# Moving three groups of loads from one issuing engine's program to another's, ahead of a cast, in a fused attention and gated-MLP kernel

## Chip, core and metric

The kernel runs on one core of a Trainium2 chip. The core has a matrix engine (TensorE, PE in the profile), a vector engine (VectorE, DVE), a scalar engine (ScalarE, ACT), a general engine (GpSimd, POOL) and SyncE (SP), which here only issues transfers. Each engine runs its own instructions in order. Transfers are carried by 16 DMA engines that all the issuing engines share; the profile calls the queue that POOL fills q0 and the one that SP fills q1. The metric is the device time in microseconds (us) of one execution. Before the change it was 238.27 us, the median of three runs (238.08 to 239.02).

## What is computed

Eight batches of grouped attention (16 query heads on 4 key/value heads, 384 positions, width 64), followed by a gated layer with a mixing step over positions:

```python
scores = scale * np.matmul(q, k.transpose(0, 1, 3, 2))
attn = softmax(scores)                       # over the keys
x = np.matmul(attn, v)                       # heads side by side: 8 x 384 x 1024
h = np.maximum(x @ w_in, 0.0)                # 1024 -> 1024
u, v = h[..., :512], h[..., 512:]
v_n = (v - mean(v)) / np.sqrt(var(v) + 1e-06)
v_s = np.einsum('ts,bsd->btd', w_spatial, v_n) + b_spatial[None, :, None]
out = (u * v_s) @ w_out                      # 512 -> 1024
```

All inputs and the output are float32; the kernel computes its matrix products in 16-bit floats.

## The kernel before

Each batch is cut into six sets (three blocks of 128 query positions by two halves of the heads), and each set into three units, one for each block of 128 keys: 18 units a batch, 144 in all. A unit is a pair of score products (tile sc, line 281), whose exponentials ACT takes (aT, line 293). After three units the values are weighted (av, line 301), and DVE divides by the row sums (lines 315 and 317) into x16.

A written plan decides the order of all instructions. The loop over units emits scores and weights; `at(n, f, ...)` books an action for unit n; `pour` fills PE's time between the scores with the matrix products of the gated layer, which the generator `gated` yields one by one. From unit 21 on the loop takes three units at a time (21, 24, 27, ...), so an action booked for 29 is emitted in the block that begins at 27, and one booked for 30, 31 or 32 in the block that begins at 30. Within one block the order of the bookings holds. Each engine then runs what was emitted for it in that order, and waits where its data isn't there.

The gated layer of one batch has these products: pv (line 357, the half that is normalised), pu (438, the half that gates), psp (457, the mixing over positions, which reads the turned spatial weights wsT16), and po (496, the output, which reads w_out16 and the gated tile gT). Between them POOL normalises (vn, line 401) and multiplies u by the mixed v (gT, line 474).

Inputs come as follows:

- `load_k`, `load_v`, `load_q` (lines 116 to 134) bring a batch's keys, values and queries in float32. A batch's queries are two tiles (j = 0, 1) of three blocks of positions each; `ts` says which blocks a load takes, so that the first block, ts = (0,), can come ahead of the "late" ones, (1, 2). The last argument is the engine that issues the transfer, SP if none is given.
- `cast_k`, `cast_v`, `cast_q` (lines 182 to 208) make 16-bit copies, mostly on POOL.
- `k_send`, `q_send` (lines 248 to 262) turn these copies by transposing transfers that SP issues; `x_send` (line 338) does the same with a batch's x16 and `send_spatial` (line 585) with the spatial weights. For the first two batches PE turns k and q itself.
- `load_w_in` and `load_w_out` (lines 161 to 171) are issued by POOL and change the type on the way, so 1 MB of w_out16 is written in two halves of 512 KB.
- `load_spatial` (line 566) brings the bias and the spatial weights on SP's queue; `cast_spatial` (line 573) makes POOL lay out the bias (line 575) and cast the weights in three steps (line 580).

`behind_rest` (line 630, booked for unit 3) is a run of POOL work for the batches ahead, with `cast_spatial` and `send_spatial` at its end. The third batch (b = 2 in the code) is the first whose keys and queries are turned by transfers. Its first score unit is unit 36, and it needs the late query blocks from unit 42 on. Before the change, w_out is loaded by POOL in the block of unit 24, the values and the late queries of the third batch by SP in the blocks of 27 and 30, and their casts stand in the blocks of 33 and 36.

Of the kernel before, what the change touches and what calls it, by code (L numbers as in the profile page):

```python
# [18 lines left out]
def kernel(  # L19
# [18 lines left out]
    DM = moe_w_in.shape[0]  # L38
    DFF = moe_w_in.shape[1]
    DH = DFF // 2  # L40
# [31 lines left out]
    pool, dve, act, sp = nc.gpsimd, nc.vector, nc.scalar, nc.sync  # L72
# [32 lines left out]
    def stage_tile(n, b, j=None):  # L105
        shape = [P, 2, NT, G * D] if n == "q" else [P, HKV, NT * D]
        t = ld.tile(
            shape, FP32, name=f"{n}32_{b}_{j}", tag=f"{n}32", bufs=5 if n == "q" else 2
        )
        stage[n, b, j] = t  # L110
        return t

    def part(src, t, lo, hi, eng):
        eng.dma_start(t[:, lo:hi, :], src[lo:hi].rearrange("h (p t) d -> p h (t d)", t=NT))
# [4 lines left out]
    def load_v(b, eng=sp):  # L119
        part(v[b], stage_tile("v", b), 0, HKV, eng)  # L120

    def part_q(b, j, hs, ts, eng):
        h0, h1, t0, t1 = hs[0], hs[-1] + 1, ts[0], ts[-1] + 1
        eng.dma_start(  # L124
            stage["q", b, j][:, h0:h1, t0:t1],
            q[b, 8 * j + 4 * h0 : 8 * j + 4 * h1].rearrange(
                "(h i) (c t r) d -> (i c) h t (r d)", i=G, t=NT, r=G
            )[:, :, t0:t1],
        )

    def load_q(b, j, eng=sp, ts=(0, 1, 2)):
        if ts[0] == 0:
            stage_tile("q", b, j)
        part_q(b, j, (0, 1), ts, eng)
# [33 lines left out]
    def load_w_out(lo, hi):  # L168
        pool.dma_start(
            w_out16[:, :, lo:hi], moe_w_out[:, lo:hi].rearrange("(m p) f -> p m f", p=P)  # L170
        )
# [401 lines left out]
    def cast_spatial():  # L573
        b32, ws32 = spatial32["b"], spatial32["w"]
        pool.tensor_copy(
            bias_bc.rearrange("a (t r c) -> a t r c", t=NT, r=G),
            b32.rearrange("a (c t r) -> a t r c", t=NT, r=G),
        )
        for tt in range(NT):
            pool.tensor_copy(  # L580
                ws16[:, :, tt].rearrange("p s (r c) -> p s r c", r=G),
                ws32[:, tt].rearrange("p (c s r) -> p s r c", s=NT, r=G),
            )
# [10 lines left out]
    def at(n, f, *args):  # L594
        todo.setdefault(n, []).append((f, args))
# [34 lines left out]
    def behind_rest():  # L630
        load_q(1, 1, pool)
        load_v(1, pool)
        cast_q(0, 1, pool, (2,))
        load_w_in(0, 0, 4)
        load_w_in(0, 4, 8)
        new_spatial()
        pool.memset(spatial32["b"][:, 0:1], 0.0)
        pool.memset(spatial32["w"][:, 0, 0:1], 0.0)
        load_spatial(sp)
        cast_k(1, pool)  # L640
        load_k(2, pool)
        cast_q(1, 0, pool)
        load_q(2, 0, pool, (0,))
        cast_q(1, 1, pool, (0,))
        cast_q(1, 1, pool, (1, 2))
        load_q(2, 1, pool, (0,))
        cast_v(1, pool)
        cast_spatial()
        send_spatial()
# [32 lines left out]
    at(24, q_send, 2, 0, 0, 1)  # L682
    at(26, cast_q, 2, 1, pool, (0,))
    at(26, q_send, 2, 1, 0, 1)
    at(26, load_w_out, 0, DH)
    at(26, load_w_out, DH, DM)
    at(29, load_q, 2, 0, sp, (1, 2))
    at(29, load_v, 2)
    at(31, load_q, 2, 1, sp, (1, 2))
    at(36, cast_v, 2, pool)  # L690
    for j, n in ((0, 34), (1, 36)):
        at(n, cast_q, 2, j, pool, (1, 2))
        at(n + 1, q_send, 2, j, 1, NT)
    at(36, load_k, 3)
# [345 lines left out]
```

## Time and profile before

| | |
|---|---|
| median of three runs | 238.27 us (238.08 to 239.02) |
| the profiled execution | 238.65 us |
| its span, first to last instruction | 237.1 us |
| granted clock of PE | 1.00 |
| PE busy | 230.4 us (97% of the span) |
| ACT busy | 170.0 us (72%) |
| DVE busy | 143.8 us (61%) |
| POOL busy | 102.2 us (43%) |
| DMA | 47.48 MB, mean 200 GB/s |

Busy time is the time in which an engine has an instruction at work; issuing transfers and waiting are not counted. A line of the timeline has the start, the duration, the engine, the line of code, the operation and what it writes from what it reads; in brackets stands how long the engine sat idle before it, and what ended that. The chain of waits is followed back from the last instruction, and lists what released each step. The DMA view of a stretch lists, for each queue, the packets that started in it, their megabytes, and the time that they took as a share of 16 engines; its last lines list the issues of that stretch with the time from issue to landing.

Around the change, POOL lays out the bias at 25.08 us, casts the spatial weights from 29.44 us and issues w_out at 34.14 us. SP issues the turn of the spatial weights at 31.94 us, the first x turn at 33.99, the third batch's k at 35.33, its first query blocks at 37.00 and 40.80, its late queries and values at 42.44, 43.09 and 47.04, and the turns of the late queries at 50.10 and 53.61.

### The profile page before, as it was taken

To read this page: it belongs to the slowest core of one execution; us is meant where nothing else is said; L and a number is where in the kernel's file an instruction comes from. 1 tells how busy PE (TensorE), PEld (TensorE's weight loads), DVE (VectorE), ACT (ScalarE), POOL (GpSimd) and SP (SyncE) were. 2 spreads that over 40 slices of the span, in tenths; PEclk is the share of its full clock that TensorE was granted. 3 is DMA by queue.
4 is the path that set the end of the run, shared out by engine and by line. 5 is a ranking of instruction groups with operands and counts; after the bars stand their busy time and mean duration, and the time that the engine had idled before them with its cause. 6 is when DMAs were issued, how large, how long until landed. Compare 5 with 4: busy or idle time off the path is not lost.

```text
span 237.1 us, 5954 instructions
## 1 busy us (share of the span) xinstructions
PE 230.4 (97%) x2317; PEld 124.3 (52%) x2317; DVE 143.8 (61%) x382; ACT 170.0 (72%) x350; POOL 102.2 (43%) x149
## 2 busy tenths in 40 slices
PE   7899999999999999999999999999999999999993
PEld 6555655545554545555464555554465455545542
DVE  2668774676447674566646576376744667367561
ACT  2899989959897869977797776986697776401212
POOL 3489493642556442275045800575032500460740
PEclk9999999999999999999999999999999999999999
DMA  6999959999999999699988899479912543240266
GB/s 186 289 300 308 275 152 160 169 317 260 296 211 237 258 351 171 214 199 309 188 257 214 241 214 294 68 271 158 255 27 44 114 164 79 48 177 0 86 229 222
DMA packets 67757, 47.48 MB, mean 200 GB/s; under 512 B 48368, under 2 KB 60576, under 8 KB 67728
## 3 DMA queue, kind: packets, MB, share of 16 engines
q1 hardware_dynamic: 62800, 39.86, 68.9%
q0 software_dynamic: 3952, 6.42, 12.3%
q10 hardware_dynamic: 976, 0.82, 1.1%
q8 instruction: 18, 0.29, 0.5%
q14 instruction: 11, 0.09, 0.1%
HBM read 25.95 MB, written 12.58 MB: 163 GB/s over the span
## 4 chain that ended last, share of the span: by engine, by line
PE 91%; DMA 4%; DVE 2%; issue 0%; ACTq 0%; ACT 0%
PE pu L438 18%; PE pv L357 17%; PE po L496 17%; PE sc L281 15%; PE av L301 14%; PE psp L457 7%; DMA q<-in_q_dram 2%; DMA qT<-q 2%; PE qps L240 1%; PE xps L334 1%; DVE x L317 1%; DVE qT L218 0%; DVE osb L218 0%; DVE q L208 0%; ACTq L124 0%
## 5 line engine op out<-in xcount | busy, mean ns | idle before, releaser
L293 ACT ACTIVATE aT<-sc 128x512 f16<-128x512 f32 x288 | 147.5, 617 | 31.4 <-PE sc L281 30.8
L301 PEld LDWEIGHTS <-aT 128*128 128x128 f16 x1152 | 47.0, 97 | 17.3 <-issue 2.3
L357 PE MATMUL pv<-w_in,xt 128*128 128x512 f16 x192 | 51.0, 380 | 0.1
L301 PE MATMUL av<-v,aT 128*128 128x65 f16 x1152 | 50.5, 193 | 0.1
L496 PE MATMUL po<-w_out,gT 128*128 128x512 f16 (+2 forms) x200 | 50.5, 371 | 0.0
L438 PE MATMUL pu<-xt,w_in 128*128 128x384 f16 x256 | 49.9, 327 | 0.0
L401 POOL TENSOR_SCALAR vn<-vr,rstd,nmr 128x512 f16<-128x512 f32 x23 | 17.6, 779 | 67.0 <-DVE nmr L396 45.6
L474 POOL TENSOR_TENSOR gT<-vs,uT 128x384 f16<-128x384 f32 x31 | 32.4, 1058 | 31.8 <-DVE r_all L315 16.9
L317 DVE TENSOR_TENSOR x<-av,r_all 128x256 f16<-128x256 f32 x96 | 40.7, 424 | 3.3
L281 PE MATMUL sc<-qT,kT 64*128 64x512 f16 x288 | 41.5, 380 | 0.3
L315 DVE RECIPROCAL r_all<-av 128x4 f32<-128x4 f32 x96 | 17.1, 178 | 40.6 <-PE av L301 40.3
L218 DVE COPY osb<-po 128x512 f32<-128x512 f32 (+2 forms) x39 | 26.1, 669 | 16.3 <-PE po L496 16.3
L438 PEld LDWEIGHTS <-w_in 128*128 128x128 f16 x256 | 22.1, 98 | 17.1 <-issue 5.5
L449 ACT ACTIVATE uT<-pu 128x384 f16<-128x384 f32 x32 | 15.8, 495 | 16.0 <-PE pu L438 15.8
L496 PEld LDWEIGHTS <-gT 128*128 128x128 f16 x200 | 17.6, 98 | 17.1 <-issue 3.3
L357 PEld LDWEIGHTS <-xt 128*128 128x128 f16 x192 | 15.8, 97 | 17.8 <-issue 5.5
L281 PEld LDWEIGHTS <-kT 64*128 64x128 f16 x288 | 10.9, 94 | 23.5 <-issue 11.9
L457 PE MATMUL psp<-wsT,vn 128*128 128x384 f16 x96 | 22.2, 327 | 0.0
L469 DVE TENSOR_TENSOR vs<-psp,bias_bc 128x384 f32<-128x384 f32 x32 | 17.6, 552 | 7.1 <-PE psp L457 6.9
L371 DVE TENSOR_SCALAR vr<-pv 128x512 f32<-128x512 f32 x24 | 16.4, 682 | 8.4 <-PE pv L357 8.3
L203 POOL CAST q<-q 128x768 f16<-128x768 f32 x22 | 17.6, 830 | 7.9 <-issue 4.3
L383 DVE BATCH_NORM_STATS2 stats<-vr 128x6 f32<-128x512 f32 x24 | 16.4, 685 | 0.1
(55 smaller groups left out, 103.2 us busy)
## 6 DMA issues: line engine op xcount, KB each, us to landing
out_dram<-osb SPq DMA_DIRECT2D x20, 512.0 KB, 3.9
q<-in_q_dram SPq DMA_DIRECT2D x10, 768.0 KB, 5.7
v_None<-in_v_dram SPq DMA_DIRECT2D x6, 384.0 KB, 7.0
w_in<-in_moe_w_in_dram POOLq DMA_DIRECT2D x4, 512.0 KB, 9.8
k_None<-in_k_dram SPq DMA_DIRECT2D x5, 384.0 KB, 3.8
out_dram<-osb SPq DMA_DIRECT2D x7, 256.0 KB, 2.5
q<-in_q_dram POOLq DMA_DIRECT2D x2, 768.0 KB, 7.6
w_out<-in_moe_w_out_dram POOLq DMA_DIRECT2D x2, 512.0 KB, 9.5
```

The lines of the kernel that those rows point to most:

```text
L203: eng.tensor_copy(t16[:, :, :, hh, :], src[:, hh])
L218: (act.copy if eng is act else dve.tensor_copy)(o, i)
L281: nc.tensor.matmul(sc, kTs[b][rows, j, kt * P : (kt + 1) * P], qTs[b, j][rows, qt].rearrange("p (r i c) -> p i r c", r=G, i=G), start=True ...
L293: act.activation(a, sc, AF.Exp, scale=scale)
L301: nc.tensor.matmul(av[:, i * (D + 1) : (i + 1) * (D + 1)], aT[:, kt, hh, i * P : (i + 1) * P], v1[b % 2][:, 2 * j + hh, kt, 0 : D + 1], st ...
L317: dve.tensor_tensor(x16s[b][:, qt, c : c + 256].rearrange("p (i d) -> p i d", i=G), o[:, :, 0:D], r.to_broadcast([P, G, D]), ALU.mult,)
L357: nc.tensor.matmul(pv, xts[b][:, kt, st * P : (st + 1) * P], w_in16[:, kt, DH:DFF], start=(kt == 0), stop=(kt == NK - 1),)
L401: (dve if b == 0 and st == 1 else pool).tensor_scalar(vn, v_r.pop((b, st)), rstd[:, st : st + 1], nmr[:, st : st + 1], op0=ALU.mult, op1=A ...
L438: nc.tensor.matmul(pu[:, 0:S], w_in16[:, kt, m * P : (m + 1) * P], xts[b][:, kt, :], start=(kt == 0), stop=(kt == NK - 1),)
L457: nc.tensor.matmul(psp[:, 0:S], v_n[b, st][:, m * P : (m + 1) * P], wsT16[:, st, :], start=(st == 0), stop=(st == NT - 1),)
L474: pool.tensor_tensor(gT, vs, uT, ALU.mult)
L496: nc.tensor.matmul(po[:, 0:width], gTs[b][:, m, tt * P : (tt + 1) * P], w_out16[:, m, c0 : c0 + width], start=(m == 0), stop=(m == NM - 1),)
```

## The change

```diff
@@ cast_spatial
             bias_bc.rearrange("a (t r c) -> a t r c", t=NT, r=G),
             b32.rearrange("a (c t r) -> a t r c", t=NT, r=G),
         )
+        load_w_out(0, DH)
+        load_w_out(DH, DM)
+        load_v(2, pool)
+        load_q(2, 0, pool, (1, 2))
         for tt in range(NT):
             pool.tensor_copy(
                 ws16[:, :, tt].rearrange("p s (r c) -> p s r c", r=G),
@@ the bookings of the third batch
     at(24, q_send, 2, 0, 0, 1)
     at(26, cast_q, 2, 1, pool, (0,))
     at(26, q_send, 2, 1, 0, 1)
-    at(26, load_w_out, 0, DH)
-    at(26, load_w_out, DH, DM)
-    at(29, load_q, 2, 0, sp, (1, 2))
-    at(29, load_v, 2)
-    at(31, load_q, 2, 1, sp, (1, 2))
-    at(36, cast_v, 2, pool)
-    for j, n in ((0, 34), (1, 36)):
+    at(26, load_q, 2, 1, pool, (1, 2))
+    at(30, cast_v, 2, pool)
+    for j, n in ((0, 31), (1, 36)):
         at(n, cast_q, 2, j, pool, (1, 2))
         at(n + 1, q_send, 2, j, 1, NT)
     at(36, load_k, 3)
```

Four transfers are now issued by POOL between the layout of the bias and the casts of the spatial weights: both halves of w_out (POOL issued them before, too, in the block of 24), the third batch's values, and the late blocks of its first query tile. The late blocks of the second query tile are issued by POOL where w_out stood. SP loses its three loads. The cast of the values goes from the block of 36 to that of 30, the cast of the first query tile's late blocks and their turn from 33 to 30. The second query tile's late cast and turn stay where they were, in the block of 36. No instruction of PE, ACT or DVE is added, removed or moved.

## The prediction

> **What bounds the kernel now.** I read the page's busy line first, then busy time by stretches, then the chain of waits. TensorE (PE) is busy for 230.4 of 237.1 us. In stretches of 2 us it is full from 32 us on, with three exceptions (columns: PE, PEld, DVE, ACT, POOL busy, clock, DMA share, GB/s):
>
> ```profile
> PE 230.4 (97%) x2317; PEld 124.3 (52%) x2317; DVE 143.8 (61%) x382; ACT 170.0 (72%) x350; POOL 102.2 (43%) x149
> ```
> ```profile
> 50.00:52.00 2.00, 1.89 (x21) 0.95 (x18) 1.93 (x6) 1.63 (x4) 0.90 (x2) 1.00 1.13 357
> ...
> 54.00:56.00 2.00, 1.88 (x29) 1.02 (x24) 1.62 (x5) 2.00 (x6) 0.00 (x0) 1.00 0.76 204
> 56.00:58.00 2.00, 1.95 (x20) 1.07 (x20) 1.40 (x5) 2.00 (x6) 0.78 (x2) 1.00 1.17 328
> ```
>
> These three hold 0.28 us of idle. Starts tell more than modelled ends: the last output matmul at 50.53 is followed at 51.02 by the third batch's first av (0.49 us, where its neighbours stand 0.22 apart), which waits for POOL's cast of v; the scores at 55.08 start 0.31 us after the last av, about 0.19 over the usual; four smaller gaps between 54.5 and 56.3 hold some 0.3. Together **0.75 us**, all that faster third-batch data can give. The granted clock is 1.00 there. The chain of waits agrees on the place but overstates the size, because during those 4.94 us PE did other work:
>
> ```profile
> 42.33 0.49 PE psp L457 x3
> ...
> 45.87 1.08 PE pv L357 x5
> ...
> 50.10 4.94 DMA qT<-q
> 55.08 1.13 PE sc L281 x6
> ```
>
> So there is little to win and much to lose: whatever PE needs later than today is added in full. The due times in the PE timeline are 42.16 for the turned spatial weights (wsT, first psp), 45.70 for the turned x, 48.10 for the third batch's kT and qT.
>
> **The change, part by part.** POOL's timeline (start, us, what, idle before):
>
> ```profile
> 25.08 0.87 POOL L575 COPY bias_bc<-spatial 128x384 f32<-128x384 f32 x1
> 29.44 2.47 POOL L580 CAST ws<-spatial 128x384 f16<-128x384 f32 x3 [3.49 <-DMA spatial<-in_moe_w_spatial_dram]
> ...
> 34.14 1.50 POOL L169 DMA_DIRECT2D w_out<-in_moe_w_out_dram  x2
> ```
>
> *Issuing on POOL.* Four issues now stand between the bias copy and the weight casts: two of w_out (1.50 us), one of v (0.78 us at 13.97), one of q (0.71 us at 21.10), sum 2.99. POOL sits idle there for 3.49 us, waiting for the spatial weights, so the issues end near 28.95, before the weights land, and cost 0. If the weights landed at once they would cost 2.99 on wsT. At 34.14 the two w_out issues become one of q: 0.75 us less on POOL. SP loses three issues (0.58, 0.48, 0.58 = 1.64 us at 42.44, 43.09, 47.04); its transposes of x and q stand closer together. PE is not waiting for those issues: 0.
>
> *The casts moved.* Cast of v (0.83 us) moves from 50.14 and the first late q cast (1.17) from 48.91 to just behind the normalisation, which ends at 40.89. This adds a wait: with data late, the gating multiplies (gT, from 43.57) queue behind it on POOL, and the first output matmul at 47.96 behind them. 2.00 us of casts fit in the 2.68 us of idle there, if data is in by about 41.5; if data comes at 45, gT slips by 3.4, of which its lead over PE (the last of four ends at 47.45, PE reads it near 49.3) covers 1.8. The price is 0 to 1.6; I take 0, because the next point delays psp, and so gT, more. The turn of q, sent at 50.10 today and landing at 55.04, can go about 5 us sooner; the stalls at 51.0 and 55.1 go: -0.75, range 0 to -0.75, as nothing else idles there. The second late q part comes from POOL at about 33.4 instead of SP at 47.04; its cast keeps its place (52.41, 1.44 us of wait gone) and PE needs its turn only at 59.61: 0. Nothing is late next, since PE is full behind these stalls.
>
> *The bytes.* This is what I think decides. The w_out transfers move from 34.14 to about 26, with v and both late q parts right behind them on POOL's DMA queue (q0): 1.0 MB written plus 1.31 MB (0.39 + 2 x 0.52). They wait in that queue behind loads that drain near 31. So they run from 31 on, beside the turn of wsT (on SP's queue, q1), issued at 31.94. Today w_out starts after that turn. What the turn does alone, in 33 to 35 us (packets, MB, share; then issues with us to landing):
>
> ```profile
> q1 hardware_dynamic: 1184, 0.30, 77.6%
> ...
> wsT<-ws SPq DMA_TRANSPOSE x1, 4.2
> xt<-x SPq DMA_TRANSPOSE x1, 6.5
> ```
>
> and beside w_out, in 37 to 40 us, then in 40.25 to 44.25 us:
>
> ```profile
> q0 software_dynamic: 450, 0.45, 112.2%
> q1 hardware_dynamic: 39, 0.00, 1.7%
> ```
> ```profile
> q0 software_dynamic: 533, 0.53, 90.8%
> q1 hardware_dynamic: 541, 0.14, 37.6%
> ```
>
> Alone, a turn moves 592 packets of 256 bytes a us; beside w_out 135, one for each packet of w_out (133 a us). (A turn's packets are its bytes by 256: 1152 for wsT, 1024 for x, 768 for kT.) The kT turn, issued at 35.33, thus landed 11.2 us after its issue, where wsT took 4.2.
>
> The estimate for wsT: w_out has 1024 packets (1 MB at 1 KB); from 31.0 to 33.1, when the turn's data starts, it moves 2.1 x 150 = 315 (150 from the 450 in 3 us). The other 709 take 709/133 = 5.3 us, to 38.4, in which wsT moves about as many and has some 440 left. Then 1.31 MB of v and q: q loads alone move 1.36 MB in 16.5 to 20 us, 389 GB/s, so 3.4 us; at some 4 KB a packet they are 320 packets, so 320 of wsT's go between (320/592 = 0.5 us), to 42.3; the last 120 take 0.2: data done at 42.5. From last data to landing is about 1.35 us for wsT today, and 3.3 for the x turn beside w_out (data gone by 37.25, landed 40.5). Near the first, since q0 is empty by then: **44.4**. PE's psp, due at 42.16, stalls **2.2 us**. Bounds: wsT landing as today (36.15, stall 0) and 46.5 as kT did behind all of w_out (4.3). Behind it, x needs 1024/592 = 1.7 us more and lands near 46.5 to 47 (due 45.70 + 2.2 = 47.9), kT and qT follow by 49 (due 50.3): no second stall.
>
> The Trainium skill, "DMA: Bandwidth & Descriptors", section "Queues, rings and completion order", says that an engine takes turns between queues by whole packets, typically 9 to 17 descriptors, before it switches. If a turn of wsT were 13 of its 256-byte pieces, 1152 would need 89 turns, the landing would be near 37, and the time that of the first rival below. The 533 against 541 of today speak for one record against one.
>
> The same section says that a completion's increment lands only after every earlier write of that engine, across its queues. The 3.3 us of the x turn agree with it; by it alone wsT would land not before the writes of v and q, and the sum would be that of the second rival.
>
> **Sum.** 2.2 - 0.75 = +1.45 us. The profiled execution took 238.65 us (span 237.1, 1.55 around it), 0.38 above the median of the runs, so 240.1 on its terms and 238.27 + 1.45 = **239.7** on the median's.
>
> **Rivals.**
> - *The turn is in time.* Point: wsT lands before 42.16. For it: today's slack is 6 us, and an engine may give the turn several packets for one of q0's where q0 holds q and v. Against: the 135 packets a us. Then only the saving is left: 238.27 - 0.75 = 237.5; not slower. Chance 0.25.
> - *The turn lands behind everything.* A landing of 45.8 to 46.5, with x then near 48: stall 3.6 to 4.3, less 0.75: 241.1 to 241.8. For it: the 3.3 us tail and kT's 11.2 us. Against: q0 should be empty by 43. Chance 0.15.
> - *The change does not do what it says.* The third batch's data comes sooner, but its turns still queue behind the earlier ones on SP, so the stalls at 51 and 55 stay; wsT in time: 238.3. Chance 0.06.
> - *POOL's new wait.* wsT in time, v or q late, gT held up to 1.6: 238.3 to 239.1. Chance 0.04.
>
> **Chances and range.** The forecast has 0.50, alone 238.6 to 241.0 (landing 43.3 to 45.7). A difference of 0.5% (1.19 us, beyond 237.08 or 239.46) is about what a measurement of this kernel tells from no change. Slower: 0.37 of the forecast's 0.50 and the second rival's 0.15: 0.52. Faster needs more than the 0.75 us that the gaps hold: 0.05, out of the first rival. Same: the rest, 0.43. The range takes in the first rival below and most of the second above: 237.3 to 242.0.
>
> **What would show it.** Right: wsT's turn landing some 12 us after its issue instead of 4.2; an idle PE ahead of the first psp, near 42 to 44; q1 with about 135 packets a us in 33 to 38; no gaps near 51 and 55 (moved by the stall). POOL's casts of the spatial weights should still start near 29.4. Wrong: wsT landed by 42, PE full through 40 to 58, or casts of the weights that start late because the issues take longer than 0.75 us each.

## The result, and the profile after

The changed kernel takes 242.70 us (median of six executions, 240.69 to 247.56) where the kernel before took 238.42 us in its own six. The ratio is 1.0142, with a 95% interval of 1.011 to 1.0175: 1.4% slower, 241.7 us on the forecast's median. The ratio leaves out two disturbed executions, so it is below the quotient of the medians. The profiled execution took 242.29 us against 238.65, its span is 240.7 us against 237.1.

Busy time is unchanged (PE 230.5 us); the time went into waiting. PE, DVE and the other engines in the stretches around the change (columns as before):

```profile
42.00:44.00 2.00, 0.64 (x8) 0.18 (x4) 0.61 (x2) 1.69 (x4) 1.48 (x3) 1.00 1.38 110
44.00:46.00 2.00, 0.14 (x1) 0.13 (x2) 0.00 (x0) 0.63 (x2) 0.15 (x1) 1.00 1.40 158
...
50.00:52.00 2.00, 2.00 (x21) 0.97 (x21) 1.25 (x4) 1.25 (x3) 2.00 (x4) 1.00 0.97 185
...
58.00:60.00 2.00, 1.89 (x18) 0.72 (x15) 1.97 (x5) 2.00 (x6) 0.00 (x0) 1.00 1.07 230
```

PE, full before in 42 to 46, worked for 0.78 of these 4 us. The chain of waits names what it waited for:

```profile
32.58 13.14 DMA wsT<-ws
45.72 0.14 issue
45.85 0.65 PE psp L457 x3
```

The turn of the spatial weights landed 13.1 us after its issue, where it took 4.2. Laid beside each other instruction by instruction, the two traces of PE stand 0.33 us apart from 16.5 us on (a wait for w_in in this execution, in which the change has no part), 3.69 from the first psp, 3.42 from the third batch's first av, and 3.4 to the end: **+3.36** at the first psp, **-0.27** at the av. In POOL's timeline the new issues cost nothing:

```profile
26.36 1.51 POOL L169 DMA_DIRECT2D w_out<-in_moe_w_out_dram  x2
27.84 0.78 POOL L114 DMA_DIRECT2D v_None<-in_v_dram  x1
28.61 0.72 POOL L124 DMA_DIRECT2D q<-in_q_dram  x1
30.10 2.45 POOL L584 CAST ws<-spatial 128x384 f16<-128x384 f32 x3 [0.77 <-DMA spatial<-in_moe_w_spatial_dram]
```

They end at 29.33, and POOL still waits 0.77 us for the weights. What the DMA queues moved in 33 to 36 us (nothing on q1), in 36.5 to 38.5 us, then in 42.5 to 45 us:

```profile
q0 software_dynamic: 603, 0.60, 121.5%
```
```profile
q0 software_dynamic: 223, 0.53, 96.2%
q1 hardware_dynamic: 193, 0.05, 18.1%
```
```profile
q1 hardware_dynamic: 444, 0.11, 140.8%
q0 software_dynamic: 24, 0.08, 8.3%
```

In the first stretch the turn, though issued at 32.58, moves nothing beside w_out. In the second it again gets about one packet for each of q0's. In the third q0 is all but empty, and still SP's queue moves 178 packets a us instead of 592. Not all of these can be wsT's: q1 had started 936 packets by 42.5 us, wsT's turn has 1152, and the x turn is next in that queue.

### The profile page after: what moved, and what is told of

Its sections match the earlier page's. It is cut to its first block, busy times and chain, and to the rows that moved or that the text cites. A ratio compares the mean times of both kernels' runs of the same rounds, so it can differ in the third digit from the quotient of the medians.

```text
span 240.7 us, 5955 instructions
## 1 busy us (share of the span) xinstructions
PE 230.5 (96%) x2317; PEld 124.2 (52%) x2317; DVE 143.1 (59%) x382; ACT 170.1 (71%) x350; POOL 104.4 (43%) x152
## 4 chain that ended last, share of the span: by engine, by line
PE 85%; DMA 11%; DVE 1%; SPq 1%; issue 0%; POOL 0%
PE po L496 17%; PE pv L357 17%; PE pu L438 16%; PE sc L281 14%; PE av L301 13%; PE psp L457 7%; DMA wsT<-ws 5%; DMA w_in<-in_moe_w_in_dram 4%; DMA v_None<-in_v_dram 2%; PE xps L334 0%; PE qps L240 0%; DVE x L317 0%; SPq L114 0%; DVE osb L218 0%; DVE vr L371 0%
## 5 line engine op out<-in xcount | busy, mean ns | idle before, releaser
L293 ACT ACTIVATE aT<-sc 128x512 f16<-128x512 f32 x288 | 147.6, 618 | 34.3 <-PE sc L281 33.5
L301 PE MATMUL av<-v,aT 128*128 128x65 f16 x1152 | 50.5, 193 | 0.0
L496 PE MATMUL po<-w_out,gT 128*128 128x512 f16 (+2 forms) x200 | 50.5, 371 | 0.0
L438 PEld LDWEIGHTS <-w_in 128*128 128x128 f16 x256 | 22.1, 98 | 17.1 <-issue 5.5
L496 PEld LDWEIGHTS <-gT 128*128 128x128 f16 x200 | 17.6, 98 | 17.1 <-issue 2.8
```

The lines of the kernel that those rows point to most:

```text
L293: act.activation(a, sc, AF.Exp, scale=scale)
L301: nc.tensor.matmul(av[:, i * (D + 1) : (i + 1) * (D + 1)], aT[:, kt, hh, i * P : (i + 1) * P], v1[b % 2][:, 2 * j + hh, kt, 0 : D + 1], st ...
L438: nc.tensor.matmul(pu[:, 0:S], w_in16[:, kt, m * P : (m + 1) * P], xts[b][:, kt, :], start=(kt == 0), stop=(kt == NK - 1),)
L496: nc.tensor.matmul(po[:, 0:width], gTs[b][:, m, tt * P : (tt + 1) * P], w_out16[:, m, c0 : c0 + width], start=(m == 0), stop=(m == NM - 1),)
```

## The experiments

**Theory.** A DMA engine takes a packet from each queue in turn, and turns follow one another on SP's queue; so a turn is late by the packets that POOL's queue holds ahead of it and beside it. **Rivals:** POOL's own time ahead of the casts (place); w_out alone, because it converts its type (kind); the volume alone, whatever its packets and order; and, for the spread of the times, PE's clock. The table has each kernel's median and its ratio to the kernel before on the same chip; "turn" is the time of wsT's turn from issue to landing, "PE waits" the long waits of PE between 40 and 60 us in the profiled execution (e10's was 5.4 us slower than its median).

| kernel | turn, us | PE waits, us | median, us | ratio, 95% interval |
|---|---|---|---|---|
| before | 4.2 | none | 238.42 | |
| changed | 13.1 | psp 3.2 | 242.70 | 1.0142, 1.011 to 1.0175 |
| e1, w_out back | 6.4 | none | 238.86 | 1.0030, 1.0003 to 1.0057 |
| e2, w_out alone ahead | 6.9 | none | 238.33 | 0.9995, 0.9974 to 1.0016 |
| e3, all behind the casts | 11.7 | psp 1.4, pv 0.7 | 239.97 | 1.0061, 1.0025 to 1.0098 |
| e4, changed, idle filled | 14.9 | filled, psp 1.3 left | 243.25 | 1.0200, 1.0158 to 1.0243 |
| e5, e3 in 2 KB packets | 17.1 | psp 5.4 | 245.29 | 1.0262, 1.0213 to 1.0311 |
| e6, e3 in 512 B packets | 7.0 | pv 2.8 | 243.52 | 1.0206, 1.0150 to 1.0262 |
| e7, w_out ahead, rest at 34 | 12.2 | psp 1.0, pv 8.8 | 250.50 | 1.0416, 1.0356 to 1.0476 |
| e8, changed, small ones first | 14.7 | psp 3.9 | 244.42 | 1.0198, 1.0137 to 1.0259 |
| e9, e7 with ACT issuing | 14.1 | psp 3.3 | 243.86 | 1.0200, 1.0138 to 1.0262 |
| e10, psp doesn't need the turn | 16.0 | pv 3.9 | 240.51 | 1.0084, 1.0050 to 1.0119 |
| e11, e5, idle filled | 15.2 | filled | 244.46 | 1.0236, 1.0171 to 1.0301 |
| e12, casts sooner alone | 3.7 | po 4.4 | 245.06 | 1.0281, 1.0232 to 1.0329 |

**e1: w_out back where it was.**

```diff
-        load_w_out(0, DH)
-        load_w_out(DH, DM)
...
     at(26, load_q, 2, 1, pool, (1, 2))
+    at(26, load_w_out, 0, DH)
+    at(26, load_w_out, DH, DM)
```

> Theory (bytes): what delays the turn of the spatial weights is the volume that stands ahead of it on POOL's DMA queue, most of it w_out. With w_out back behind that turn, only 0.91 MB of v and q stay ahead, which the queue moves by about 34; the turn, issued near 32.5, lands by 39, before PE needs it at 42.4. No stall there, the gap before the third batch's first av (0.27 us) stays gone: 237.7 to 238.4, within 0.5% of before. Rival (place): any transfer that POOL issues ahead of its casts of the spatial weights delays them or the turn by the same 3 us: 240.5 or more, and PE idle ahead of the first psp.

The turn landed at 37.1, PE was full through 42 to 54, and the gap before the av was gone. POOL's place ahead of the casts is not what costs: two issues stand there still. The gain of 0.27 us is in the profile, but not in the time, which is 0.3% above before and above what was expected. That is less than the 0.5% that a measurement of this kernel tells from no change.

**e2: w_out alone ahead** (the first hunk's two `load_w_out` lines in the kernel before, and its two bookings at 26 gone).

> Only the two w_out transfers go in front of the casts of the spatial weights; v, late q, their casts and turns are as before. Theory (bytes): w_out alone drains by 38 to 40 (its second half landed at 40.3 in the changed kernel), and the turn of the spatial weights, with 1152 packets, lands at 40 to 42, just before PE needs it: stall 0 to 0.5, the old gaps at 51 and 55 stay, 238.3 to 239.2. Rival (kind of transfer): w_out, which converts its type, is the whole cause, and v and q add nothing: wsT lands near 45, stall 2.5 to 3.4, 241 to 242.5.

The turn landed at 39.8, a little sooner than expected, and PE had no wait at its use, near 43.1 in that execution. w_out alone is harmless, as v and q alone are in e1: it takes both, 1.9 MB ahead of the turn and 0.5 MB beside it. The kind alone is not the cause.

**e3: all four issues right behind the casts of the spatial weights.**

```diff
-        load_w_out(0, DH)
-        load_w_out(DH, DM)
-        load_v(2, pool)
-        load_q(2, 0, pool, (1, 2))
         for tt in range(NT):
...
+        load_w_out(0, DH)
+        load_w_out(DH, DM)
+        load_v(2, pool)
+        load_q(2, 0, pool, (1, 2))
```

> All of the change, but the four transfers are issued right behind the casts of the spatial weights instead of in front of them. Theory (bytes ahead of the turn): the turn of the spatial weights then starts before w_out does and lands by 38; no stall at the first psp. The x turn that follows takes the delay (landing 44 to 47, due 45.9): stall 0 to 1. 237.8 to 239.3. Rival (order does not matter, the same 2.3 MB compete with the same turns): 241 or more.

Half missed: w_out (issued at 31.44) and the turn (31.51) now start together, so the turn has no lead, and lands at 43.2 instead of by 38; the time is 0.7 us above the expected range. The x turn took the delay that was expected (a wait of 0.7). The six us in which both run, 34 to 40, give the cleanest sight of the alternation (packets, MB, share):

```profile
q0 software_dynamic: 926, 0.93, 91.4%
q1 hardware_dynamic: 914, 0.23, 29.6%
```

**e5 and e6: the same place, other packets.** w_out by rows (512 packets of 2 KB), then in four quarters by columns (2048 of 512 bytes):

```diff
 # e5
+        m0, m1 = lo * NM // DM, hi * NM // DM
-            w_out16[:, :, lo:hi], moe_w_out[:, lo:hi].rearrange("(m p) f -> p m f", p=P)
+            w_out16[:, m0:m1], moe_w_out[m0 * P : m1 * P].rearrange("(m p) f -> p m f", p=P)
 # e6
-        load_w_out(0, DH)
-        load_w_out(DH, DM)
+        for c in range(0, DM, 256):
+            load_w_out(c, c + 256)
```

> As the kernel with the four transfers behind the casts (239.97 us, wsT's turn from 31.5 to 43.2), but w_out comes in two halves by rows instead of by columns, so the same 1 MB is 512 packets of 2 KB instead of 1024 of 1 KB. Theory (an engine takes one packet from each queue in turn): the turn of 1152 packets has moved only some 512 when w_out is through, near 41, and needs v's and q's packets and more for the rest: wsT lands at 44.5 to 46, the first psp stalls 2 to 3.5, 241 to 242.5. Rival (the queues share by time or bytes): wsT lands near 43.2 as before, 240.0.

> The same placement, but w_out in four quarters by columns: 2048 packets of 512 bytes, four issues (POOL spends 1.5 us more there). Theory (one packet from each queue in turn): the turn moves its 1152 packets beside as many of w_out's and is done before w_out is: wsT lands at 40.5 to 42.3, no stall or under 0.4 at the first psp; the x turn behind it may still be late by up to 1.5: 238.3 to 240. Rival (share by time or bytes): wsT lands near 43.2 or later, the stall of 1.2 stays.

The landing follows the packets: 47.4 with 2 KB, 43.2 with 1 KB, 38.1 with 512 bytes, for the same megabyte; both changes go the expected way, further than expected. The counts in 38 to 40 us of e5 and in 33 to 35 us of e6 show why: one for one at either size.

```profile
q0 software_dynamic: 174, 0.36, 94.0%
q1 hardware_dynamic: 176, 0.05, 19.1%
```
```profile
q0 software_dynamic: 451, 0.23, 84.8%
q1 hardware_dynamic: 417, 0.11, 40.0%
```

The rival (shares by time or bytes) falls. Both times missed their ranges, e5's by 2.8 us and e6's by 3.5. e6 saves no time: the x turn, next on SP's queue, then landed 14.6 us after its issue, PE waited 2.8 us for it, and its granted clock was 0.50 for 3.4 us behind. The stall had moved.

**e8: v and q first, w_out behind them** (the four added lines in another order).

> The changed kernel with the order of the four issues changed: v and q first, w_out behind them, the same 1.9 MB ahead of the turn. Theory (one packet from each queue in turn): v and q, in packets of 4 KB, pass before the turn starts, and beside w_out's packets of 1 KB it moves about twice as many a us as beside theirs: wsT lands at 42 to 44, stall 0 to 1.5, 238.5 to 240.5. Rival (volume ahead alone): wsT lands at 45 to 46.5 as in the changed kernel, 241 or more.

Here my theory missed the landing and the volume had it right: 46.2. The alternation was as expected (438 packets of the turn beside 442 of q0 in 36 to 39), and by 42.5 us SP's queue had started 1220 packets, more than the 1152 of this turn. So by count the turn's packets were out nearly when the theory has them out, and the landing came 3.7 us later. In that tail, 42.5 to 45.75, SP's queue moved 604 more packets, 186 a us, beside 18 of q0. A slow tail stands in the changed kernel as well. What causes it is open: packets a us explain the first part of the delay, not the last 2 to 3 us.

One thing goes with this tail. In the changed kernel and in e4, e5, e8, e9, e10 and e11 wsT's turn landed within 0.5 us of the last load of late queries (load at 45.3 and turn at 45.7 in the changed kernel, 46.0 and 46.2 in e8). In e1, e3, e6 and e7 it landed 1 us or more before that load. No run moves that load alone, so what it adds is not known.

**e7 and e9: w_out ahead of the casts, v and late q at w_out's old place, issued by POOL, then by ACT.**

```diff
         load_w_out(DH, DM)
-        load_v(2, pool)
-        load_q(2, 0, pool, (1, 2))
...
+    at(26, load_v, 2, pool)
+    at(26, load_q, 2, 0, pool, (1, 2))
     at(26, load_q, 2, 1, pool, (1, 2))
```

> Only w_out goes in front of the casts of the spatial weights (wsT's turn landed at 39.8 that way); v and the late q parts are issued by POOL where w_out stood before, in the block of unit 24, and their casts and turns are as early as in the changed kernel. Theory (bytes ahead of the turn): wsT lands by 41, x and k by 46, no stall; the gap of 0.27 us before the third batch's first av is gone: 237.7 to 238.4, not to be told from before. Rival (the total of POOL's transfers in 26 to 45 decides, wherever they stand): a stall of over 1 us at psp or at the x turn, 239.3 or more.

> As the kernel with w_out ahead of the casts and v and late q behind them (250.5 us; there v and q, issued by POOL at 34 to 36, crawled until 51 to 56 and the x turn landed 21.7 us after its issue), but ACT issues v and late q, at the same place. Theory (POOL's own queue beside turns is what crawls): the loads on ACT's queue land within 10 us, the x turn by 46, 238 to 239.5. Rival (any second queue beside the turns does it): the x turn lands at 50 or later, 245 or more.

e7 was meant as the better kernel and is the worst. wsT's turn landed at 43.2, not by 41, and PE waited 1.0 us for it and 8.8 for the x turn. Its rival (239.3 or more) holds, but says nothing of this size: in 40 to 50 us the queues moved

```profile
q1 hardware_dynamic: 801, 0.20, 75.8%
q0 software_dynamic: 123, 0.47, 43.8%
```

which is 67 GB/s for all, and the x turn landed 21.7 us after its issue. With ACT issuing the same loads (its queue is q10), 37 to 42 us had

```profile
q10 hardware_dynamic: 813, 1.08, 76.2%
q1 hardware_dynamic: 812, 0.21, 25.5%
```

and the crawl was gone; the x turn landed at 46.3. That the queue makes the crawl is not shown, though: e9's loads were also issued 2 us sooner, and in the changed kernel v and q passed on POOL's queue without a crawl (q0's 0.53 MB in 36.5 to 38.5 us). e9 is no cure, and its time missed the expected 238 to 239.5: its loads were issued at 32.3 to 33.5, soon enough to alternate with the turn of wsT, which landed at 45.7. A third queue beside the turns costs as the second does.

**e10: which turn is next.** The first batch's psp reads the cast weights as they are.

```diff
-                wsT16[:, st, :],
+                ws16[:, st].rearrange("p t c -> p (t c)") if b == 0 else wsT16[:, st, :],
```

> The changed kernel, but the first batch's mixing over positions reads the cast weights before they are turned, so that its psp does not wait for the turn, which is still made; that batch's result is not the reference's. Theory (turns follow one another, so the stall moves to the next one): the x turn, which landed at 48.0, is due at 46.0: a stall of 1.5 to 3 ahead of pv at 46 in place of the 3.4 ahead of psp, 240 to 241.5. Rival (wsT's turn is the only late one): no stall, 238 to 238.7.

240.51: the time fits the theory, 0.8% above before though nothing waits for wsT's first use. The one profiled execution took 245.95 us, so the size of its wait is not that of the median, but its place is the one that the theory names:

```profile
50.49 2.31 PE L357 MATMUL pv<-w_in,xt 128*128 128x512 f16 x5 [3.86 <-DMA xt<-x]
```

**e4 and e11: the clock.** Products of zeros ahead of the first psp, in the changed kernel (60) and in e5 (80):

```diff
         psp = bank([P, 512], FP32, f"psp_{b}_{m}")
+        if (b, m) == (0, 0):
+            for _ in range(60):
+                nc.tensor.matmul(psp[:, 0:P], zero16, zero16, start=True, stop=True)
```

> The changed kernel with 60 products of zeros (128 columns, 3.4 us) on PE just ahead of the first psp, in the place where PE stood idle; they write the bank that the first psp clears. Theory (clock): some of the runs of the changed kernel had a mean clock of 0.98 to 0.99, and the times spread from 240.7 to 247.6, because PE sits idle for 3 us; with that idle time filled the clock is 1.00 in every run and the times stand within 1.5 us of each other, near 241 to 242.5, with wsT's turn landing as late as in the changed kernel. Rival (the DMA race itself varies from run to run): the spread stays, the clock is 1.00 or not, as before.

> As the kernel with w_out in packets of 2 KB behind the casts (245.3 us; PE waits 5.2 us for wsT, and the granted clock is 0.5 for the 3.4 us after it), with 80 products of zeros (128 columns, 4.5 us) on PE just ahead of the first psp, in its idle time. Theory (idle time lowers the clock): the granted clock is 1.00 behind the wait as well, the 1.1 us that PE lost there are back: 243.6 to 244.5. Rival (the clock falls for another reason): 0.5 for some us again, 245 or more.

In e5 PE stood idle for 5.4 us and then ran at half the granted clock; e11's PE was kept busy. Stretches 44 to 47.5 and 47.5 to 50.5, first of e5, then of e11:

```profile
44.00:47.50 3.50, 0.00 (x0) 0.00 (x0) 0.00 (x0) 0.18 (x1) 1.17 (x2) 0.95 0.89 176
47.50:50.50 3.00, 2.93 (x20) 1.76 (x21) 1.32 (x4) 0.00 (x0) 1.05 (x1) 0.50 0.77 162
```
```profile
44.00:47.50 3.50, 3.50 (x65) 3.44 (x63) 0.00 (x0) 1.03 (x3) 1.18 (x2) 1.00 1.27 143
47.50:50.50 3.00, 3.00 (x30) 1.57 (x29) 2.00 (x5) 0.82 (x2) 1.74 (x2) 1.00 0.63 131
```

From the first psp to the third batch's first av e5 took 10.00 us and e11, whose clock stayed at 1.00, 8.58. So a long wait costs more than itself. The median of e11 is 0.8 us lower than that of e5, but the intervals of their ratios overlap, so the traces show this better than the times. In the changed kernel two of the four executions that the ratio rests on had a mean clock of 0.99; in e4 none was under 0.996. But e4's theory missed: its times still spread over 3.3 us (241.89 to 245.18) and are not lower, so that spread is not the clock's, and e4's rival (the transfers vary) fits better. The 60 products did not fill the whole wait; 1.3 us of it were left.

**e12: the casts sooner, without the loads** (in the kernel before, only the bookings 36 to 30 and 34 to 31).

> The kernel before with the third batch's two casts and the turn booked sooner (30, 31 and 32), and no load moved. Theory (POOL's new wait is free only while the data comes early): the cast of v stands ahead of the first batch's gating multiplies and waits for v, which landed at 50.0; gT starts near 51 instead of 43.6, the last of four ends near 55 where PE reads it at 49.3 to 49.7 today: a stall of 4 to 6 ahead of or within the first po, 242 to 244.5. Rival (the casts moved sooner are harmless, since POOL is busy for 43% only): 238 to 238.8.

POOL's timeline shows the wait that the prediction priced for late data:

```profile
48.87 0.82 POOL L191 CAST v<-v_None 128x768 f16<-128x768 f32 x1 [8.49 <-DMA v_None<-in_v_dram]
...
50.78 3.67 POOL L474 TENSOR_TENSOR gT<-vs,uT 128x384 f16<-128x384 f32 x4
```

The gating waits behind the casts, PE waits 4.7 us for it in two pieces, and its clock is 0.5 for 3.4 us from 52.7 on. The time lies 0.6 us above the expected range, which had no term for the clock. An engine that is busy for 43% of the time still stops everything when an instruction that waits stands ahead of one that is due.

## Why the prediction was right, and where its sizes were off

- **What bounds.** Right: PE is full, and the whole 3.36 us at psp stayed to the end.
- **POOL's issues cost 0.** Right: 2.97 us of issues in front of a wait, 0.77 us of which is left.
- **POOL's new wait costs 0.** Right for this change: the cast of v waited 0.43 us and that of q 0.52, and both were done at 44.2, before wsT landed. The bound of 1.6 was worked out for data at 45; in e12, where the cast of v had to wait until 48.9, the price was 4.7 us and the clock.
- **The turn beside the bytes.** Right in its mechanism for most of the way (e1, e2, e5, e6) and in which instruction waits; e8 leaves the end of the turn unexplained. The term "wsT lands at 44.4, stall 2.2" is the one that was mis-sized: it landed at 45.7, stall 3.36. Three parts of that term. The turn's first packets came after 36 instead of at 33.1 (issue at 32.58, 0.64 later than before, 2.28 us long instead of 1.41, and none moved while w_out had 200 packets a us, not 150). One for one held while both queues were full. And the last packets were slow: by count the turn's 1152nd packet started between 43.5 and 44.0 (1105 and 1209 of q1), where the prediction has the data done at 42.5. From there to the landing it took about 2 us, as the prediction has it (1.9). The term's upper bound of 4.3 held. Two slips in the working changed little: 0.39 + 2 x 0.52 is 1.43 MB, not 1.31, which at its 389 GB/s is 0.3 us more; and POOL's issue of the second late q part takes w_out's place at 34.14, not 33.4 (it came at 34.79).
- **The saving of 0.75 us.** The step that failed: only the 0.27 us ahead of the av went. The gap at 55 stayed (58.6 to 59.3 now), though that turn of q landed 6 us ahead of use. The prediction gave it to the turn because the chain did; behind the turn stood another wait. The chain of waits of the changed kernel there:

```profile
57.74 0.19 DVE r_all L315
57.96 0.42 DVE x L317
58.38 0.61 DVE vr L371
58.99 0.04 issue
59.03 0.60 PE sc L281 x3
```

  By it the scores at 59.03 follow DVE's read of pv (vr), which no load moves. Whether a buffer that DVE frees is the reason was not tried. A chain shows one of two waits that end together.
- **The sum.** 3.36 - 0.27 = 3.1, where the forecast has 2.2 - 0.75 = 1.45; with the 0.33 of the start it is the 3.4 of PE's end. The result, 241.7 on the forecast's median, lies with its second rival (241.1 to 241.8), whose point was a landing of 45.8 to 46.5. So the forecast alone (238.6 to 241.0) missed: it had the stall too small and the saving too large, and both errors go the same way. The range held because it took in that rival, to which the prediction gave 0.15; the plain median of 242.70 lies above its 242.0. That is part luck.
- **Not foreseen: the clock.** An execution in which the wait grows can lose more behind it, which may be part of the spread up to 242.8 us; the profiled execution, with a wait of 3.2 us, kept 1.00 throughout. The Trainium skill, "TensorE: Matmul & The Clock Gate", section "Part 1: The HAM clock gate (the "warmup" mystery)", says that an idle window of about 3.4 us halves the clock and that a busy one restores it, the windows running freely. The traces agree in the length: 0.50 for 3.41 us in e5, e6, e9 and e12, for 6.83 in e8, for 10.24 in e7 (6.1 of them inside its wait of 8.8), never in e11. They add that the window need not be idle throughout: in e8 the clock fell 2.2 us into the wait, and it was 0.50 behind e6's wait of 2.8 us too, while the changed kernel's 3.2 us left it at 1.00.

No version beats the kernel before: e2 equals it, and the 0.27 us to be had is less than a measurement tells.

## What to carry to other kernels

A transfer that is issued early, at no cost to its issuer, is not free: look at what else its queue will run beside, and compare due times, not queue lengths. Here 1.9 MB that PE first reads at 47.8 us (w_out) and 51.0 (v) were put ahead of a turn that it reads at 42.2, and packets, not bytes, decided how they shared. Before the change v and the late queries stood on the turns' own queue, among the turns, and PE lost no more than 0.27 us by it. Where a wait comes near 3 us, look at the clock behind it too.

## What the runs showed of the hardware that was not expected

- Two queues that are both full share the DMA engines packet by packet, at the three packet sizes that were tried: 926 to 914 at 1 KB, 174 to 176 at 2 KB, 451 to 417 at 512 bytes. The queue that ACT fills does the same beside the turns (813 to 812 in e9). Equal counts do not tell whether an engine takes one packet from each queue at a time or several.
- A turn that is issued into a running stream of w_out moved nothing for its first microseconds (603 packets to none in 33 to 36 us of the changed kernel), though one that starts together with the stream (e3) had its share from 34 us on.
- POOL's loads of v and q beside turns fell to 123 packets in 10 us in e7, and the turns to 80 a us; the same loads from ACT's queue, issued 2 us sooner, did not. The cause is open, as is that of the slow tail of SP's queue when the other queue is almost empty (178 packets a us against 592), and of a landing that comes 3.7 us after the turn's packets are out by count (e8).
- The granted clock fell to 0.50 behind a wait of 2.8 us (e6) and stayed at 1.00 behind one of 3.2 us (the changed kernel): near 3 us the length of the wait alone does not tell.
